# Decode attention with an MLP gate on one core: 68 of the 128 row pairs of heads 28 and 29 of the output weights load through GpSimd's queue, ahead of time, on two pairs of DMA engines

## The chip, the cores and the metric

The kernel runs on one core of a Trainium2 chip. A core has five engines with instruction streams of their own: PE (TensorE, matrix multiplication), DVE (VectorE), ACT (ScalarE), POOL (GpSimd) and SP (SyncE, which here does nothing but issue loads and stores), and 16 DMA engines that move data between the chip's memory (HBM) and the core's on-chip memory. SP, ACT and POOL can issue transfers, each into a queue of its own; the DMA engines work these queues off. Time is in microseconds (us) of the device; the metric is the median over several executions, lower is better.

## What is computed

One token passes through a block: a layer norm, attention of 32 heads over the last 4096 positions of a key and a value cache, and, beside it, a small MLP whose output gates the attention's.

```python
def _A_ref(x, k_cache, v_cache, wq, wo):          # x (1,1,512), caches (1,32,32768,128)
    W = min(4096, max(256, Sk // 4))              # 4096
    q = (x @ wq).reshape(B, Sq, Hq, Dh).transpose(0, 2, 1, 3)
    k = k_cache[:, :, Sk - W:, :]
    v = v_cache[:, :, Sk - W:, :]
    scores = einsum("bhqd,bhkd->bhqk", q, k) * (Dh ** -0.5)
    o = einsum("bhqk,bhkd->bhqd", softmax(scores), v)
    return o.transpose(0, 2, 1, 3).reshape(B, Sq, Hq * Dh) @ wo    # wo (4096, 512)
...
xn = _layernorm(x)
return x + _A_ref(xn, ...) * _silu(_B_ref(xn, ...))
```

Everything is bfloat16. The caches' windows are 32 MB each for K and V and must be read once: they are nearly all of the kernel's traffic.

## The kernel before

**Groups and steps.** The 32 heads are worked in eight groups of four (`G`). One group's keys are 4096 KB, laid out as 128 partitions by 128 chunks by 128 numbers, so that each partition gets one piece of 32 KB; one group's values likewise. The loop runs over ten steps `s`. In step `s` the keys of group `s` are loaded and multiplied with the query, half of them on DVE (`k_vector`: a product and a reduction, four parts) and half on PE (`k_turn` transposes, ACT copies the result out, `k_scores` multiplies). The softmax of group `s-1` follows (`sm_max`, `sm_turn`, `sm_exp`), and in the same step the values of group `h = s-2` are multiplied with its probabilities (`v_wide`, `v_turn`, `v_add`, `v_out`). `sm_den` and `sm_rden` make the reciprocal `rden` of a group's softmax sum; in step 6 that is group 4's.

**The output weights.** `wo` has a row block of 128 rows by 512 for each head. Heads 0 to 15, 16 to 23 and 24 to 27 are loaded as three blocks and used by `y_wide`. Heads 28 to 31 belong to the last group, whose output comes last; their rows are loaded into the tile `wo_rows` (128 partitions, 4 heads, 512 numbers, so 1 KB for a head in each partition), by two loads of two heads each (`load_rows`). They are the last loads in SP's queue, behind the last group's values. `y_head` multiplies them, four small matmuls a head, into `y_ps`.

**Who issues what.** SP issues nearly all loads, in the order of the program (`load`, line 76). A load into a buffer that is still read waits for that reader, and everything that SP is to issue later waits behind it. There are three buffers for keys and two for values. ACT issues the query weights and the input at the start. `mark` issues tiny loads: `marks` of k rows of 32 bytes for k = 1, 3, 5, 7 behind the last keys and for 9, 11, 13, 15 behind the `wo` blocks. GpSimd issues no transfers; its last instruction is the second `ln_rstd`, at 12 us.

**The tail.** Steps 8 and 9 have no keys. In step 9 the last values come in three cuts (chunks 0 to 64, 64 to 96 and 96 to 128). PE's order there is written by hand: `v_open`, three `warm` matmuls on zeros, `v_wide` on the first cut, the block of heads 24 to 27 (`ox_pick`, `y_wide`), `v_wide` on the second cut, `v_turn`, the sum of the earlier heads into `y_ps` (`rows_add`), `v_part` on the third cut (32 matmuls), then, once DVE has scaled the result (`v_out`), `y_head` for heads 28 to 31: 16 matmuls. DVE multiplies by the gate, adds the input, and SP stores 512 numbers.

`warm` matmuls write a PSUM tile that nobody reads.

Of the kernel before, what the change touches and what calls it, by code (L numbers as in the profile page):

```python
# [8 lines left out]
P = 128  # L9
BF16 = mybir.dt.bfloat16  # L10
FP32 = mybir.dt.float32
# [7 lines left out]
G = 4  # L19
LAG = 2  # L20
K_BUFS = 3
V_BUFS = 2
LATE = 7


@with_exitstack
def kernel(
# [14 lines left out]
    nc = tc.nc  # L42
# [3 lines left out]
    _, H, Sk, Dh = A_k_cache.shape  # L46
# [17 lines left out]
    small = ctx.enter_context(tc.tile_pool(name="small", bufs=1))  # L64
# [10 lines left out]
    def load(dst, src):  # L75
        return tc.keep_in_program_order(nc.sync.dma_start(out=dst, in_=src))  # L76
# [8 lines left out]
                        in_=A_wq.rearrange("(a b c) n -> b a (c n)", a=4, c=KC))  # L85
# [27 lines left out]
    zero_bf = const.tile([P, P], BF16, name="zero_bf")  # L113
# [95 lines left out]
    for b in range(2):  # L209
        zeros(qr[b][:])  # L210
        for c in range(KC):
            wc = wq_sb[:, c, :].rearrange("p (g a d) -> p g a d", a=G, d=Dh)
            for a in range(G):
                nc.tensor.matmul(qr[b][32 * a:32 * a + 1], lhsT=xq_bf[:, c:c + 1], rhs=wc[:, 4 * b:4 * b + 4, a, :],  # L214
                                 start=False, stop=(c == KC - 1), skip_group_check=True)
    nc.scalar.copy(out=q_row[:, 0:4, 0, :], in_=qr[0][:])
    nc.vector.tensor_copy(out=q_row[:, 4:8, 0, :], in_=qr[1][:])  # L217
    for b in range(2):
        qb_ps = ps_tr.tile([P, 4, Dh], FP32, tag="pt", name="qb_ps")
        nc.tensor.matmul(qb_ps[:], lhsT=sel[:].rearrange("k b a -> k (b a)"), rhs=q_row[:, 4 * b:4 * b + 4, 0, :],  # L220
                         start=True, stop=True)
        nc.scalar.copy(out=q_bc[:, 4 * b:4 * b + 4, :], in_=qb_ps[:])
    for b in range(2):
# [5 lines left out]
        for t in range(2):  # L229
            rows = slice(64 * t, 64 * t + 64)  # L230
            nc.scalar.copy(out=q_pair[rows, 4 * b:4 * b + 4, :, G * t:G * t + G].rearrange("p g l a -> p g a l"),
                           in_=qt_ps[rows].bitcast(BF16).rearrange("p g (a m l) -> p g a m l", a=G, l=2)[:, :, :, 0, :])
# [4 lines left out]
    for j in range(KC):  # L237
        for c in range(KC):
            nc.tensor.matmul(hs_ps[:, j:j + 1], lhsT=w2_sb[:, c, j::4],
                             rhs=shifted_bf[:, c:c + 1], start=(c == 0), stop=(c == KC - 1))  # L240
# [30 lines left out]
    for i in range(11):  # L271
        n = P if i < 10 else 96
        terms.append((a_bf[0:n, i % 3, i // 3:i // 3 + 1], w4_sb[0:n, i, :]))
    for i, (col, w) in enumerate(terms):
        r = 32 * (i % 4)
        nc.tensor.matmul(hr_ps[r:r + 1].rearrange("r j n -> r (j n)"), lhsT=col, rhs=w, start=False,
                         stop=(i >= len(terms) - 4), skip_group_check=True)
# [34 lines left out]
    st = {}  # L312

    def nd(g):
        return 64 if g == 0 or g >= LATE else 80

# [85 lines left out]
    def sm_rden(g):  # L402
        s = st[g]
        s["rden"] = sm_pool.tile([P, G], FP32, tag="rden", name="rden")
        nc.vector.reciprocal(out=s["rden"][:], in_=s["den"][:])  # L405
# [4 lines left out]
    h_part = H - G  # L410
# [6 lines left out]
    def wo_row(h):  # L417
        return wo_rows[:, h - h_part, :]

    def load_rows(h, n):  # L420
        load(wo_rows[:, h - h_part:h - h_part + n, :],
             A_wo[h * P:(h + n) * P, :].rearrange("(h p) n -> p h n", p=P))

    ov = ps_o.tile([P, 4, Dh], FP32, name="ov")
    zeros(ov[:])
# [82 lines left out]
    def warm(n):  # L510
        wm = ps_s.tile([P, 4, P], FP32, tag="sT", name="wm")
        for _ in range(n):
            nc.tensor.matmul(wm[:], lhsT=zero_bf[:], rhs=zero_bf[:].unsqueeze(1).to_broadcast([P, 4, P]),
                             start=True, stop=True)

    def y_open():
        yr[0] = ps_tr.tile([P, KC, P], FP32, tag="pt", name="yr_ps")
        zeros(yr[0][:])
# [18 lines left out]
    for s in range(NG + LAG):  # L537
        h = s - LAG
        last = h == NG - 1
        kn = load_kv(k_pool, A_k_cache, s, (0, 64, CP) if s == 0 else (0, CP)) if s < NG else None  # L540
        if s == NG - 1:
            mark((1, 3, 5, 7))
        if s == LAG:
            wts_guard.__exit__(None, None, None)
            v_pool = ctx.enter_context(tc.tile_pool(name="v", bufs=V_BUFS))
            wo_blk[2] = v_pool.tile([P, 4, D], BF16, tag="wo_4", bufs=1, name="wo_4")
            wo_rows = v_pool.tile([P, H - h_part, D], BF16, tag="wo_rows", bufs=1, name="wo_rows")
        if last:
            v = load_kv(v_pool, A_v_cache, h, cuts)
            for r in (H - G, H - 2):  # L550
                load_rows(r, 2)
        elif h >= 0:
            v = load_kv(v_pool, A_v_cache, h)
        if h == 3:
            wo_24 = k_pool.tile([P, 32, D], BF16, tag="kv", name="wo_24")
            wo_blk[0], wo_blk[1] = wo_24[:, 0:16, :], wo_24[:, 16:24, :]
            load_wo(0)
        if h == 5:
            load_wo(1)
            load_wo(2)  # L560
            mark((9, 11, 13, 15))

        if s < NG:
            nb = len(batches(s))

            def keys(b0, b1):
                for b in range(b0, b1):
                    k_turn(s, kn, b)
                    if b > 0:
                        k_scores(s, b - 1)  # L570

            k_open(s)
            k_vector(s, kn, 0)
            keys(0, 2)
            if s == 7:
                v_turn(h - 1)
                v_add(h - 1)
                v_out(h - 1)
            elif s > 1:
                sm_den(s - 2)  # L580
                sm_rden(s - 2)
            elif s == 1:
                sm_max(0)
            k_vector(s, kn, 1)
            keys(2, 4)
            if s == 7:
                sm_den(h)
                sm_rden(h)
                keys(4, nb - 2)
                sm_turn(s - 1)  # L590
                keys(nb - 2, nb)
            else:
                if s > 0:
                    sm_turn(s - 1)
                keys(4, nb)
            k_scores(s, nb - 1)
            sm_own(s)
            if s == 7:
                k_vector(s, kn, 2)
                v_wide(h, v)  # L600
                sm_exp(s - 1)
                v_turn(h)
                y_open()
                k_vector(s, kn, 3)
                v_add(h)
                v_out(h)
                ox_spread(1)
                sm_max(s)
                continue
            if s > 0:  # L610
                sm_exp(s - 1)
            if h > 0:
                v_turn(h - 1)
            k_vector(s, kn, 2)
            if h >= 0:
                v_wide(h, v)
            if h > 0:
                v_add(h - 1)
                v_out(h - 1)
            if s == 6:  # L620
                ox_spread(0)
            k_vector(s, kn, 3)
            if s == 6:
                ox_pick(0)
            if s > 0:
                sm_max(s)
        elif s == NG:
            ox_pick(1)
            sm_turn(NG - 1)
            sm_exp(NG - 1)  # L630
            y_wide(1, False)
            sm_den(NG - 2)
            sm_rden(NG - 2)
            y_wide(0, False)
            warm(3)
            v_wide(h, v)
            sm_den(NG - 1)
            sm_rden(NG - 1)
            v_turn(h)
            v_add(h)  # L640
            v_out(h)
            ox_spread(2)
        else:
            v_open(h)
            warm(3)
            v_wide(h, v, cuts[1], last=False)
            ox_pick(2)
            y_wide(2, True)
            nc.scalar.copy(out=y_sum[:], in_=yr[0][:].rearrange("p j n -> p (j n)"))
            v_wide(h, v, cuts[2], cuts[1])  # L650
            v_turn(h)
            v_add(h)
            rows_add(y_ps, ind, y_sum, False)
            v_part(h, v, cuts[2], CP)
            v_out(h)
            for r in range(H - G, H):
                y_head(r)
# [36 lines left out]
```

## Time and profile before

| | us |
|---|---|
| median of three runs (193.39 to 193.83) | 193.8 |
| time of the profiled execution | 193.51 |
| its span on the core | 191.3 |
| DVE busy | 150.9 |
| PE busy | 118.0 |
| ACT busy | 89.2 |
| last `v_part` begins / first `y_head` matmul / store issued | 186.22 / 187.47 / 188.77 |

The page of a profile gives, among other things, the busy time of each engine, a row of 40 equal slices with the busy share of the DMA engines in tenths, the queues (packets, MB, share of the time of 16 DMA engines), and the chain of waits: from the last instruction back to what released it, and so on. In the chain's list each line is a start, a length and what ran. The timeline lists instructions in order: start, length, engine, line of the code, operation, what it writes and reads, and in brackets how long the engine had been idle and what ended that. An "x15" counts instructions. The trace also holds a record of every DMA packet, with its queue, size, start and length.

### The profile page before, as it was taken

Reading aid. Unit: us, or ns where it says so; the run is one execution under the profiler, and the core shown is the slowest. Engines: PE = TensorE matmul, PEld = TensorE weight load, DVE = VectorE, ACT = ScalarE, POOL = GpSimd, SP = SyncE. Lnnn points to the kernel's source line nnn. Section 1 sums busy time; section 2 is a strip of 40 time slices with the busy share of each in tenths; the row PEclk is TensorE's granted clock in tenths of the full one; section 3 lists DMA queues with packets and bytes.
Section 4 is the critical chain, followed back from the end, with each engine's and each line's share of the span. In section 5 each row is a group of like instructions: output and inputs, shape, how many; then the busy total and the mean of one; then the engine's idle time right before and its main releaser. Section 6 shows DMA issues by size and latency. Waiting matters only on the chain.

```text
span 191.3 us, 2847 instructions
## 1 busy us (share of the span) xinstructions
PE 118.0 (62%) x1159; PEld 74.9 (39%) x1159; DVE 150.9 (79%) x175; ACT 89.2 (47%) x191; POOL 2.3 (1%) x11
## 2 busy tenths in 40 slices
PE   1554753989825368256845772680989289739762
PEld 0430222767614334143434442540864077313321
DVE  1660159979999999999999999999999999980111
ACT  2001370887794076427364564542575148734120
POOL 2110000000000000000000000000000000000000
PEclk9999695555755557955695588557555858975995
DMA  6999999999999999999999999999999998999990
GB/s 204 440 444 403 441 418 428 439 439 437 432 440 439 425 435 432 432 439 439 428 432 425 425 421 404 452 432 435 439 439 433 435 432 379 472 425 404 416 367 26
DMA packets 4700, 79.02 MB, mean 413 GB/s; under 512 B 752, under 2 KB 1360, under 8 KB 1616
## 3 DMA queue, kind: packets, MB, share of 16 engines
q1 hardware_dynamic: 4392, 74.65, 91.5%
q10 hardware_dynamic: 296, 4.20, 5.1%
q8 instruction: 9, 0.15, 0.3%
q14 instruction: 3, 0.02, 0.0%
HBM read 78.84 MB, written 0.00 MB: 412 GB/s over the span
## 4 chain that ended last, share of the span: by engine, by line
DVE 46%; DMA 43%; PE 6%; ACT 2%; issue 1%; SPq 1%; ACTq 0%; DVEq 0%
DMA kv<-in_A_k_cache_dram 31%; DVE S L329 28%; DVE prod L327 15%; DMA kv<-in_A_v_cache_dram 10%; DMA x_bf<-in_A_x_dram 2%; PE pt L345 2%; ACT kt L348 2%; PE ov L433 1%; PE sT L356 1%; DVE m L372 1%; SPq L76 1%; DVE S L370 1%; PE oT L467 1%; DVE mx L380 1%; PE ot_ps L450 0%
## 5 line engine op out<-in xcount | busy, mean ns | idle before, releaser
L329 DVE TENSOR_REDUCE S<-prod 128x20 f32<-128x2560 bf16 (+1 forms) x32 | 86.0, 2686 | 1.1
L348 ACT COPY kt<-pt 128x1024 bf16<-128x1024 bf16 x52 | 51.2, 1013 | 39.6 <-PE pt L345 37.9
L345 PE MATMUL pt<-ident_f,kv 128*128 128x128 f32 x208 | 46.8, 376 | 10.5 <-DMA kv<-in_A_k_cache_dram 10.5
L327 DVE TENSOR_TENSOR prod<-kv,q_bc 128x2560 bf16<-128x2560 bf16 (+1 forms) x32 | 45.4, 1417 | 3.8 <-DMA kv<-in_A_k_cache_dram 3.6
L345 PEld LDWEIGHTS pt<-ident_f,kv 128*128 128x128 f32 x208 | 34.3, 196 | 14.0 <-DMA kv<-in_A_k_cache_dram 9.7
L356 PE MATMUL sT<-q_pair,kt 128*128 128x8 bf16 x416 | 19.5, 170 | 15.6 <-ACT kt L348 15.5
L356 PEld LDWEIGHTS <-kt 128*128 128x128 bf16 x416 | 16.5, 105 | 26.7 <-ACT kt L348 25.7
L433 PE MATMUL ov<-kv,pT 128*16 128x512 bf16 x248 | 22.4, 523 | 1.2 <-DMA kv<-in_A_v_cache_dram 1.2
L394 ACT ACTIVATE pT<-S,mb 128x128 bf16<-128x128 f32 x32 | 14.0, 574 | 0.3
L378 PE MATMUL mt_ps<-ident_f,m 128*1 128x128 f32 x8 | 2.9, 360 | 17.3 <-DVE rden L405 16.8
L439 ACT COPY ov_sb<-ov 128x512 f32<-128x512 f32 x8 | 4.7, 586 | 18.1 <-PE ov L433 18.1
L433 PEld LDWEIGHTS <-pT 128*16 128x16 bf16 x248 | 6.8, 110 | 13.8 <-issue 12.0
L365 ACT ACTIVATE own<-sT,par 128x48 f32<-128x48 f32 (+1 forms) x32 | 7.5, 355 | 3.7 <-PE sT L356 3.7
L450 PE MATMUL ot_ps<-ident_f,ov_sb 128*128 128x128 f32 x32 | 7.5, 377 | 2.7 <-ACT mb L390 1.7
L217 DVE CAST q_row<-qr_ps 128x512 bf16<-128x512 f32 x1 | 0.7, 691 | 9.9 <-PE qr_ps L214 9.9
L394 ACT ACTIVATION_READ_ACCUMULATOR pT<-S,mb 128x1 f32 x32 | 8.3, 260 | 0.0
L378 PEld LDWEIGHTS mt_ps<-ident_f,m 128*1 128x1 f32 x8 | 0.6, 80 | 17.8 <-DVE rden L405 17.1
L405 DVE RECIPROCAL rden<-den_ps 128x4 f32<-128x4 f32 x8 | 1.4, 175 | 7.1 <-PE den_ps L400 7.1
L387 PE MATMUL mb_ps<-md,par_t 5*128 5x4 f32 x16 | 4.1, 323 | 4.1 <-DVE md L382 4.1
L450 PEld LDWEIGHTS ot_ps<-ident_f,ov_sb 128*128 128x128 f32 x32 | 4.8, 188 | 3.8 <-ACT mb L390 2.1
L261 ACT ACTIVATE a_row<-a_ps 128x384 bf16<-128x384 f32 x1 | 0.5, 490 | 12.1 <-remote 12.1
L387 PEld LDWEIGHTS mb_ps<-md,par_t 5*128 5x128 f32 x16 | 3.6, 275 | 5.1 <-PE sT L356 3.7
(122 smaller groups left out, 81.9 us busy)
## 6 DMA issues: line engine op xcount, KB each, us to landing
kv<-in_A_k_cache_dram SPq DMA_DIRECT2D x7, 4096.0 KB, 25.5
kv<-in_A_v_cache_dram SPq DMA_DIRECT2D x7, 4096.0 KB, 30.6
wq_sb<-in_A_wq_dram ACTq DMA_DIRECT2D x1, 4096.0 KB, 17.5
kv<-in_A_k_cache_dram SPq DMA_DIRECT2D x2, 2048.0 KB
wo<-in_A_wo_dram SPq DMA_DIRECT2D x1, 2048.0 KB
kv<-in_A_v_cache_dram SPq DMA_DIRECT2D x1, 2048.0 KB
kv<-in_A_v_cache_dram SPq DMA_DIRECT2D x2, 1024.0 KB, 17.6
w_sb<-in_B_w_dram SPq DMA_DIRECT2D x1, 1376.0 KB, 10.1
```

Of the source, the lines that this page charges most:

```text
L327: nc.vector.tensor_tensor(out=prod[:, 0:m, :], in0=kn[:, rows, :], in1=q_bc[:, g:g + 1, :].to_broadcast([P, m, Dh]), op=ALU.mult)
L329: nc.vector.tensor_reduce(out=st[g]["S"][:, rows], in_=prod[:, 0:m, :], axis=AX.X, op=ALU.add)
L345: nc.tensor.transpose(pt[:, i, :], kn[:, c:c + 2, :].rearrange("p c d -> p (c d)").bitcast(FP32), ident_f[:])
L348: nc.scalar.copy(out=kts[b][:, 0:n, :], in_=pt[:, 0:n, :].bitcast(BF16))
L356: nc.tensor.matmul(st[g]["sT"][:, c:c + 2, :].rearrange("p c a -> p (c a)"), lhsT=kt[:, i, l::2], rhs=q_pair[:, g, l, :], start=(l == 0), ...
L365: nc.scalar.mul(s["own"][:, 0:m, a], s["sT"][:, 0:m, a], par[:, a:a + 1])
L378: nc.tensor.transpose(mt_ps[:], s["m1"][:], ident_f[:])
L387: nc.tensor.matmul(mb_ps[:], lhsT=par_t[:].rearrange("k b a -> k (b a)"), rhs=md[:], start=True, stop=True)
L394: nc.scalar.activation(out=s["pT"][:, :, a], in_=s["S"][:], func=ACT.Exp, scale=scale, bias=mb[:, a:a + 1], accum_out=s["sum"][:, a:a + 1])
L433: nc.tensor.matmul(ov[r:r + 4 * G], lhsT=s["pT"][:, c:c + 4, :].rearrange("p i a -> p (i a)"), rhs=v[:, c:c + 4, :], start=(i < 4), stop=( ...
L439: nc.scalar.copy(out=s["ov_sb"][:], in_=ov[:])
L450: nc.tensor.transpose(ot_ps[:, step * j:step * j + P], s["ov_sb"][:, j, :], ident_f[:])
```

## The change

A new constant `ARC = 34`. Two tiles are added, `skip` and `gate`. In step 6, after `rden` of group 4 is issued, GpSimd copies that `rden` into `gate`, and then issues five loads: a tiny one of 7 rows, 34 partitions of heads 28 and 29 (partitions 0 to 33), a tiny one of 6 rows, the next 34 partitions (34 to 67), and a tiny one of 15 rows. A tiny row is two runs of 16 bytes. SP's load of heads 28 and 29 shrinks to partitions 68 to 127; its load of heads 30 and 31 stays. In step 9 the third `warm` matmul takes as its right side the first 68 partitions of head 28's rows in place of zeros (its left side is still zeros), so that it waits for GpSimd's two larger loads.

```diff
+ARC = 34
...
-    def load_rows(h, n):
-        load(wo_rows[:, h - h_part:h - h_part + n, :],
-             A_wo[h * P:(h + n) * P, :].rearrange("(h p) n -> p h n", p=P))
+    def rows_of(h, n, p0, p1):
+        return (wo_rows[p0:p1, h - h_part:h - h_part + n, :],
+                A_wo[h * P:(h + n) * P, :].rearrange("(h p) n -> p h n", p=P)[p0:p1])
+
+    def load_rows(h, n, p0, p1):
+        load(*rows_of(h, n, p0, p1))
+
+    skip = small.tile([16, 3, 2, 16], BF16, name="skip")
+    gate = small.tile([P, G], FP32, name="gate")
+
+    def load_arcs(g):
+        tc.keep_in_program_order(nc.gpsimd.tensor_copy(out=gate[:], in_=st[g]["rden"][:]))
+
+        def step(i, k):
+            tc.keep_in_program_order(nc.gpsimd.dma_start(
+                out=skip[0:k, i, :, 0:8], in_=A_x[0, 0, :].rearrange("(k t n) -> k t n", t=2, n=16)[0:k, :, 0:8]))
+
+        step(0, 7)
+        for i, k in enumerate((6, 15)):
+            dst, rows = rows_of(H - G, 2, ARC * i, ARC * i + ARC)
+            tc.keep_in_program_order(nc.gpsimd.dma_start(out=dst, in_=rows))
+            step(1 + i, k)
...
+        return wm
...
-            for r in (H - G, H - 2):
-                load_rows(r, 2)
+            load_rows(H - G, 2, 2 * ARC, P)
+            load_rows(H - 2, 2, 0, P)
...
+                if s == 6:
+                    load_arcs(s - 2)
...
-            warm(3)
+            wm = warm(2)
+            nc.tensor.matmul(wm[:].rearrange("p j n -> p (j n)"), lhsT=zero_bf[0:2 * ARC, :],
+                             rhs=wo_rows[0:2 * ARC, 0, :], start=True, stop=True)
```

## The prediction

> **What bounds the kernel now.** The page first: its DMA row and the queues.
>
> ```profile
> PE 118.0 (62%) x1159; PEld 74.9 (39%) x1159; DVE 150.9 (79%) x175; ACT 89.2 (47%) x191; POOL 2.3 (1%) x11
> ...
> DMA  6999999999999999999999999999999998999990
> ...
> q1 hardware_dynamic: 4392, 74.65, 91.5%
> q10 hardware_dynamic: 296, 4.20, 5.1%
> q8 instruction: 9, 0.15, 0.3%
> ...
> HBM read 78.84 MB, written 0.00 MB: 412 GB/s over the span
> ```
>
> The DMA engines are at 9 tenths or more from the second slice to the end of the loads, and POOL has next to nothing to do. The mean rate over stretches says how full: 1.00 of the engines' time from 40 to 130 us at 431 GB/s, 0.99 from 130 to 185.8. So DVE's 79%, which leads the chain of waits by share, is work beside a full stream of loads; the end is set by the stream. The last part of the chain, in order of time, shows it:
>
> ```profile
> 167.70 18.47 DMA kv<-in_A_v_cache_dram
> 186.17 0.05 issue
> 186.22 1.01 PE oT L467 x32
> 187.22 0.02 issue
> 187.25 0.17 DVE o L477
> 187.42 0.04 issue
> 187.47 0.64 PE y_ps L161 x15
> 188.10 0.02 issue
> 188.13 0.30 DVE y L660
> ```
>
> Eighteen microseconds of V load (the last cut of the last group), then only what cannot start before it: 32 matmuls, the scaling, 16 matmuls with wo_rows, two DVE steps, the store.
>
> Next the packet records, below the page. A packet starts 3 or 4 ns before the one ahead of it on its engine ends, so they can be strung into 16 chains, one for each DMA engine (the records do not name engines). From 49 us on the chains have no gap; a 32 KB packet takes 1213 to 1222 ns in all of them. They end the last V cut at these times: six at 184.04 to 184.19 us, one at 185.05, one at 185.37, eight at 185.56 to 185.85. What separates them is in the records too: eight of the nine 16 KB packets of queue 8 (instruction fetches) come before that end, and the seven of them that can be placed lie one each in seven of the last eight chains; 8 KB packets of queue 14 lie in the chains that end at 185.05 and 185.37. Around a fetch the chain loses 1.4 to 1.5 us: it takes 1006 to 1098 ns where the 16 KB packets of queue 1 take 611, and the next 32 KB packet takes 1.68 to 1.76 us. **The end is set by the chains that carried a fetch, and the six others have about 1.7 us to spare.** The 32-byte packets of `mark` tell chains apart: the four that hold 0, 8, 4 and 4 of them are among the six.
>
> **The change, part by part.** The profiled execution has a span of 191.3 us and a time of 193.51; the three runs have a median of 193.8, 0.3 above it.
>
> *Removed from SP's stream:* the first wo_rows load shrinks from 128 to 60 row pairs on 15 engines: 16 rows of 1 KB on each become 8, none on the sixteenth. Rows of 1 KB start 42 to 43 ns apart in the chains, so 8 x 42.5 = 0.34 us less. It lies behind the last V cut, so it moves only what follows: the second wo_rows load, whose last packet ends at 187.21. Who waits for that? The last 16 matmuls come as four groups of four: at 187.465, 187.525, 187.695 and 187.755. Two groups of a load stand 60 ns apart, but the third, the first to need the second load, starts 170 ns after the second. So wo_rows costs 0.11 us of waiting now. It started 0.48 us after the last packet's end; 0.34 us earlier (and 0.05 later, below) it would be ready at 187.40, before `o` lets the first group go at 187.465. Gain 0.11 us. The bound from the other side, with all four groups held by the load alone, is 187.695 - 187.465 = 0.23 us.
>
> *Added on four engines:* 34 row pairs on two engines are 17 pairs, 34 KB, on each: 34 x 42.5 ns = 1.45 us. If the queue deals its rows to consecutive engines, the small loads of 7, 6 and 15 rows put the two pairs on the eighth and ninth and on the sixteenth and first, which are the four chains above (4, 4, 0 and 8 marks). They end the last V cut at 184.04 to 184.19; plus 1.45 plus the small loads gives 185.5 to 185.7, under 185.85. Cost nothing, hidden by the slow chains. The cover is thin: (185.85 - 184.19) / 34 = 49 ns a row; beyond it every ns a row costs 0.034 us at the end.
>
> The nearest rows for the price of a row: 42.5 ns back to back in queue 1; and where two queues share an engine, as q1 and q10 do from 6.2 to 21 us, packets alternate one by one and the 478 of them are lengthened by 495 ns in all, 1 ns each, at a mean of 435 GB/s. The far row is the fetch, which stops its neighbour by 0.37 to 0.66 us (queue 14) once for each packet; 34 such stops would be 13 to 22 us. I take 43 ns, because rows out of a standing queue are nearest to q10.
>
> The Trainium skill, "DMA: Bandwidth & Descriptors", section "Why a DMA increments its semaphore by 16 and not by 1", has GpSimd's queue deal to k consecutive engines from a round-robin cursor, with k the largest divisor up to 16: 2 for 34 rows, 7, 6 and 15 for the small loads, which gives these pairs if the cursor starts at the first engine; no run here shows it yet.
>
> *Small loads on all the others:* `step` puts two 16-byte packets on each engine that it touches, and every delayed chain gets two such steps. A mark (32 bytes and its 4-byte completion) adds 12 ns to a chain. Four packets and up to five completion writes at 6 ns: 0.05 us, ahead of the last V cut, so on the path: +0.05. From above, if each of the two steps stops the engine as a queue 14 packet does: 2 x 0.37 to 2 x 0.66 = 0.74 to 1.32 us. I take the low end, by the row that has small loads of one queue in another's stream: x_bf's 8-byte packets lengthened q1's by 0.86 us over 16 engines between 2.85 and 4.3 us, 0.05 each.
>
> *GpSimd's work:* it waits for `rden` of group 4:
>
> ```profile
> 138.33 0.17 DVE L405 RECIPROCAL rden<-den_ps 128x4 f32<-128x4 f32 x1
> ```
>
> then one copy (its nearest, L184, takes 0.55 us) and five issues (SP's take 0.53 each): to 141.8. Nothing else is on that engine until the end. With one row for each packet of queue 1, 34 packets pass: K7, V5, wo1, wo2 are 32 of them and end at 164.6; the rows are down by about 169. PE asks for them in the changed third `warm` matmul:
>
> ```profile
> 179.72 0.81 PE L513 MATMUL wm<-zero_bf 128*128 128x512 bf16 x3
> ...
> 181.34 1.04 PE L433 MATMUL ov<-kv,pT 128*16 128x512 bf16 x16 [0.81 <-DMA kv<-in_A_v_cache_dram]
> ```
>
> Behind it on PE stand v_wide and all the tail, but v_wide waits for V7 until 181.34 anyway, so 12 us hide the loads and 0.8 us the matmul's own wait. If the copy or the issues slow DVE (3.3 us at worst), the last pT is ready at 174.3 for a V that lands at 180.9: hidden. K7 has been issued by then (130.37). Extra waits in SP's tail (62 ns each) fit into the 0.7 us in which it waits for the store.
>
> *Sum:* -0.11 + 0.05 = -0.06 on 193.51, and 193.7 against the median.
>
> **Rivals.**
>
> *Stalls by the new queue.* An engine drops its stream for a small load as it does for a fetch. For it: queue 14's 8 KB packets took 309 to 325 ns, no more than queue 1's, yet the next packet was 0.37 to 0.66 us longer, and neither of the queues that stall is of the page's kind hardware_dynamic, as q1 and q10 are; which kind GpSimd's is, no trace here shows. Against: q10's small packets, above. It is on the path from the first stop on, since the delayed chains have no slack. Two steps at 0.5 us: +1.0, with the 0.11 gained: 194.6. If all five loads stop every engine, 5 x 0.37 = 1.85: 195.5.
>
> *The four engines become the last.* Either the rows cost over 49 ns, or a pair sits on a delayed chain (another start of the dealing, a fetch on one of the four). On a delayed chain: 185.85 + 1.45 = 187.30, +1.45, so 195.2. At 70 ns a row: 184.19 + 2.38 + 0.1 = 186.67, +0.8: 194.5. For it: the placement is nowhere in this trace. Against: four of four fit the unhit chains. The Trainium skill, same page, "Latency and other measured facts", calls engines 7 and 15 usually slower, and this specific to GpSimd's queue, whose descriptor rings share their ports; by that rule two of the four engines would be the ones to overrun, with the 194.5 of the 70 ns row, and I give it 0.05 of this rival's 0.16. In this trace, without that queue, the chains with the marks of engines 7 and 15 are among the fast six.
>
> *The rows arrive late.* If they came after 181.3, PE would stand with the whole tail behind it: about 1 us for each late us. It takes over 12 us more than worked out: 3 in 100, some 195.
>
> *Faster by more than the wait.* The last V cut itself would have to land earlier on the slow chains; the change takes no byte from ahead of it there. It needs a fetch to move away from them: ending by 193.1 or less.
>
> **Chances.** Forecast 0.46; stalls 0.26; four engines last 0.16; late rows 0.03; faster 0.09. A measurement of this kernel can tell about 0.3% (0.6 us) from no change. Faster 0.09, same 0.46, slower 0.45. The likeliest alone: 193.3 to 194.1. The range over all: 193.2 to 195.3, which takes in both main rivals' centres and leaves out the five-fold stop, rows that each stop the engine, and part of the faster case.
>
> **What would show it.** Right: the last V cut lands at 185.8 to 185.95 with 14 or more chains within the last microsecond; the third group of the last matmuls follows the second by 60 ns; the wm matmul takes no wait beyond 181.3. Stalls: 32 KB packets over 1.5 us behind 16-byte packets after 139 us on most chains. Four engines last: the latest ends of the V cut are on chains that hold 34 extra 1 KB rows. Wrong altogether: the V cut landing before 185.5.

## The result and the profile after

The changed kernel takes 195.97 us (median of four runs, 195.81 to 196.27) beside 193.69 for the kernel before (four runs, 193.39 to 193.83): 1.0122 times as long, 95% interval 1.0104 to 1.0140. It is 2.28 us slower, and it lies above the predicted range. One run of all that follow, 206.23 us in the kernel with the even partitions, was in a slow state and is left out of its ratio.

The page of the changed kernel, its DMA row and its queues, the lines that were shown of before:

```profile
PE 122.1 (63%) x1159; PEld 78.4 (40%) x1159; DVE 151.2 (78%) x175; ACT 89.4 (46%) x191; POOL 7.5 (4%) x17
...
DMA  6999999999999999999999999999999999999990
...
DMA packets 4979, 79.02 MB, mean 406 GB/s; under 512 B 1131, under 2 KB 1603, under 8 KB 1895
...
q1 hardware_dynamic: 4255, 74.51, 91.3%
q10 hardware_dynamic: 296, 4.20, 5.1%
q0 software_dynamic: 416, 0.14, 0.3%
q8 instruction: 9, 0.15, 0.3%
...
HBM read 78.84 MB, written 0.00 MB: 405 GB/s over the span
```

The same bytes come over at 405 GB/s instead of 412. A new queue, q0, has 416 packets for 0.14 MB. The rows themselves are 36 packets (below) and the tiny loads have 28 rows between them; 416 is far more, and it is 26 times 16. The queue's own packets take 0.3% of the engines' time, 0.6 us; the loss is four times that. So the loss isn't in what the queue moves. It is in what it does to its neighbours, or elsewhere.

The chain of waits of the changed kernel, its last part in order of time (start, length, what ran):

```profile
170.07 19.23 DMA kv<-in_A_v_cache_dram
189.30 0.05 issue
189.35 1.03 PE oT L485 x32
190.38 0.02 issue
190.40 0.17 DVE o L495
190.57 0.04 issue
190.62 0.63 PE y_ps L162 x15
```

The chain has the shape that it had before. From the first of the 32 matmuls to the first matmul with the output weights is 1.27 us, before 1.25. All that was lost is lost ahead of 189.35, in the stream of V. The last 8 KB packet of V ends at 188.47 us, before at 185.84; by the chain the load has landed at 189.30 (170.07 + 19.23), before at 186.17. So 2.6 us are lost up to the last packet, and 0.5 us between it and the landing.

Where in the stream? A view by stretches of time, before and then after (stretch, length, busy time of PE, PEld, DVE, ACT and POOL with instructions, granted clock of PE, share of the DMA engines, GB/s). Of before:

```profile
95.00:137.00 42.00, 23.68 (x238) 15.79 (x237) 41.19 (x33) 21.68 (x51) 0.00 (x0) 0.70 1.01 432
140.00:172.00 32.00, 21.53 (x216) 13.90 (x215) 30.30 (x36) 16.73 (x39) 0.00 (x0) 0.71 1.01 434
```

Of after:

```profile
95.00:137.00 42.00, 24.54 (x229) 15.90 (x230) 40.79 (x33) 20.78 (x50) 0.00 (x0) 0.64 1.00 429
140.00:172.00 32.00, 22.81 (x221) 15.57 (x217) 29.77 (x32) 17.41 (x39) 4.34 (x6) 0.62 1.01 405
```

Read the last two columns. From 140 to 172 us, the time in which GpSimd's loads are at work, the engines are as full as before and move 7% less: (434 - 405) / 434 of 32 us is 2.1 us of stream. And from 95 to 137 us, when GpSimd has not issued anything yet, the rate is already 429 instead of 432.

The packet records of the changed kernel, strung into 16 chains as in the prediction, say what fills the engines. This is a stretch of one chain that carries none of the rows (start in us, queue, bytes, length in ns):

```
146.818  q1  32768  1241
148.056  q0     16    11
148.063  q1  32768  1285
149.344  q0     16    11
149.351  q1  32768  1401
```

A 32 KB packet takes 1213 ns before. Here 16-byte packets of the new queue stand between SP's packets, and each 32 KB packet behind one is longer: 118 ns on the mean of 117 of them (over 1216 ns). Counted by size, q0 has 32 packets of 4096 bytes and 4 of 2048 (the rows, on four engines), 28 of 32 bytes (the tiny rows), 224 of 16 bytes, 48 of 8 and 80 of 4. **Every one of the five loads puts as many packets on each of the 16 engines as its busiest engine has**: for 34 row pairs nine packets with data on two engines, and nine of 16 or 8 bytes on each of the 14 others (called fillers from here on), and a completion on all; for a tiny load one and a completion. 2 x 10 + 3 x 2 = 26 on each engine.

Last, where the stream's stages end on the chains. The load of group 6's values ends, over the 16 chains, at 174.26 to 176.07 us before. After, three chains end it at 176.70 to 176.85 and thirteen at 177.95 to 178.43, among them, as far as the stringing tells, all four that carried rows. So the four engines are no later than the nine others, and the whole stream is late. But the rows are not hidden either. Before, seven chains end the load by 174.42, the four that were to carry rows among them; after, only three end it early. By this count the rows' engines moved by at least 3.5 us (177.95 - 174.42), where the prediction worked out 1.5 and had 1.7 to spare. Some 0.6 us of it are the moved tiles, told below.

One caution for the absolute times that follow. The part of the time that lies outside the span is 2.1 to 2.3 us in every run of the kernel before, and 1.7 to 1.9 in every run of the changed kernel and of the thirteen below, also where GpSimd loads nothing. So inside the span each of them loses some 0.35 us more than its time says (the changed kernel's median span is 194.2 us, that of the kernel before 191.2 to 191.4). No run here shows why. Kernels of the same time also differ by 0.5 us in when a stage ends. Sizes therefore come from the medians of the times and from differences within one trace.

### The profile page after: what moved, and what is told of

The parts are those of the page before. It is cut to its first block, busy times and chain, and to the rows that moved or that the text cites. A ratio compares the mean times of both kernels' runs of the same rounds, so it can differ in the third digit from the quotient of the medians.

```text
span 194.5 us, 2859 instructions
## 1 busy us (share of the span) xinstructions
PE 122.1 (63%) x1159; PEld 78.4 (40%) x1159; DVE 151.2 (78%) x175; ACT 89.4 (46%) x191; POOL 7.5 (4%) x17
## 4 chain that ended last, share of the span: by engine, by line
DVE 46%; DMA 43%; PE 6%; ACT 1%; issue 1%; SPq 1%; DVEq 0%; ACTq 0%
DMA kv<-in_A_k_cache_dram 31%; DVE S L330 28%; DVE prod L328 15%; DMA kv<-in_A_v_cache_dram 10%; PE pt L346 2%; DMA x_bf<-in_A_x_dram 2%; ACT kt L349 1%; PE ov L451 1%; PE sT L357 1%; DVE m L373 1%; DVE S L371 1%; SPq L77 1%; DVE mx L381 1%; PE oT L485 1%; PE ot_ps L468 0%
## 5 line engine op out<-in xcount | busy, mean ns | idle before, releaser
L346 PE MATMUL pt<-ident_f,kv 128*128 128x128 f32 x208 | 50.2, 399 | 10.7 <-DMA kv<-in_A_k_cache_dram 10.7
L346 PEld LDWEIGHTS pt<-ident_f,kv 128*128 128x128 f32 x208 | 37.1, 209 | 14.3 <-DMA kv<-in_A_k_cache_dram 10.3
L451 PE MATMUL ov<-kv,pT 128*16 128x512 bf16 x248 | 22.9, 531 | 2.4 <-DMA kv<-in_A_v_cache_dram 2.4
L432 POOL COPY gate<-rden 128x4 f32<-128x4 f32 x1 | 1.4, 1417 | 126.0 <-DVE rden L406 126.0
```

The lines of the kernel that those rows point to most:

```text
L346: nc.tensor.transpose(pt[:, i, :], kn[:, c:c + 2, :].rearrange("p c d -> p (c d)").bitcast(FP32), ident_f[:])
L451: nc.tensor.matmul(ov[r:r + 4 * G], lhsT=s["pT"][:, c:c + 4, :].rearrange("p i a -> p (i a)"), rhs=v[:, c:c + 4, :], start=(i < 4), stop=( ...
```

## The experiments

Thirteen kernels were run. They fall into three questions, in which order they are told here. All ratios are to the kernel before, run on the same chip in turn with them.

### Which part costs: tiny loads, the rows, the copy?

**Five loads that are all tiny.** The two loads of rows become tiny rows; SP loads all 128 row pairs.

```diff
-            dst, rows = rows_of(H - G, 2, ARC * i, ARC * i + ARC)
-            tc.keep_in_program_order(nc.gpsimd.dma_start(out=dst, in_=rows))
+            step(3 + i, 2)
...
-            load_rows(H - G, 2, 2 * ARC, P)
+            load_rows(H - G, 2, 0, P)
...
+            warm(3)
```

> Five GpSimd loads at the same place and on the same engines, but the two larger ones carry 2 rows of 32 bytes each; SP loads all of wo_rows, as before. Theory 'turns' (each packet of GpSimd's queue that takes a turn between SP's packets costs its engine some 0.05 to 0.13 us, and every engine gets as many packets as the busiest one, 26 with the change, 10 here): 10 packets of 4 to 32 bytes at about 0.05 us, so 0.4 to 0.6 us over before, 194.1 to 194.3. Theory 'loads' (a fixed cost of about 0.48 us for each GpSimd load on every engine, 2.4 us in all): as slow as the change, 195.9 to 196.1. Theory 'four engines' (the engines with the 34 KB became the last, the rest costs nothing): 193.7 to 193.8.

193.94 us, 1.0025 (1.0015 to 1.0035). The ten packets that each engine gets (160 in q0) lengthen the 32 KB packets behind them by 9 ns (4 bytes), 24 ns (8 bytes) and 14 ns (32 bytes). Five loads from this queue don't stop an engine five times. The time lies under what the theory 'turns' expected, and the kernel with the copy alone, below, takes as long, so the five tiny loads add nothing that the runs can tell.

**Half as many rows by GpSimd.** The two loads carry head 28's rows only, SP loads the rest.

```diff
-            dst, rows = rows_of(H - G, 2, ARC * i, ARC * i + ARC)
+            dst, rows = rows_of(H - G, 1, ARC * i, ARC * i + ARC)
...
-            load_rows(H - G, 2, 2 * ARC, P)
+            load_rows(H - G, 1, 2 * ARC, P)
+            load_rows(H - G + 1, 1, 0, P)
```

> The two larger GpSimd loads carry head 28 alone (34 rows of 1 KB, 17 KB on each of the four engines), SP loads the rest of head 28 and all of head 29. Turns: each larger load now makes 5 packets and a completion on every engine where it made 9 and one, so 18 in place of 26: 0.5 for the small part and 8 of 16 fillers at 0.12, 1.45 us over before, 195.0 to 195.3. Loads: five loads still, 195.8 to 196.1. Four engines: 17 KB is 0.72 us less on them, so under 194.6.

195.59 us, 1.0109 (1.0091 to 1.0127): little less than the whole change, but by another way, so that it does not answer the question. The rows are not on two pairs of engines any more. q0 has 160 packets, 22 of them of 3072 bytes: a load of 34 rows of one head is dealt three rows to an engine, over twelve engines. A 3072-byte packet takes 128 ns and makes the 32 KB packet behind it 188 ns longer, and all of these rows go to partitions 0 to 67. What that means is told with the loads that are spread over 16 engines, below.

**Other engines for the rows.** Tiny loads of 3, 6 and 3 rows move the two pairs.

```diff
-        step(0, 7)
-        for i, k in enumerate((6, 15)):
+        step(0, 3)
+        for i, k in enumerate((6, 3)):
```

> The change with small loads of 3, 6 and 3 rows in place of 7, 6 and 15: if the queue deals rows to consecutive engines, the two pairs move from the eighth and ninth and sixteenth and first engine to the fourth and fifth and the twelfth and thirteenth. The packets on each engine are as many as with the change. Turns, with the prediction's reading of the engines: the twelfth and thirteenth carry an instruction fetch each and have no slack, so the end moves by the 34 KB, 1.45 us, and by what the larger packets cost more than fillers (9 x 0.03), on top of the change's 2.3: 197.3 to 197.8. If the fillers alone made the change slow and the place of the 34 KB does not matter: 195.9 to 196.1.

197.61 us, 1.0242 (1.0175 to 1.0309; three runs of 197.50 to 197.62 and one of 200.28): by the medians 1.6 us more than the change. Group 6's values now end at 178.85, 179.24 and 179.26 us on three chains and by 178.07 on all others. The dealing follows the sizes of the tiny loads, and a pair of engines without slack costs about what the prediction worked out for it (1.45). Why three chains are that late, and not two, is open. Five chains now end the load early, by 176.92, where the change has three, as it must be if only two of the engines with rows now belong to the early seven. So the change had its rows where they were meant to be, on the engines with the most slack.

**The copy alone.** GpSimd copies `rden`, and loads nothing.

```diff
-        step(0, 7)
-        for i, k in enumerate((6, 15)):
...
-            step(1 + i, k)
...
-            load_rows(H - G, 2, 2 * ARC, P)
+            load_rows(H - G, 2, 0, P)
...
+            warm(3)
```

> GpSimd waits for rden and copies it, but issues no load; SP loads all of wo_rows, as before. All three theories: as before, 193.5 to 193.9. If GpSimd's wait and copy beside DVE were what cost the time: up to 195.9.

194.02 us, 1.0024 (1.0013 to 1.0034), the same as the five tiny loads, and over what all three theories expected. Nothing is loaded by GpSimd, and 0.42 us are gone, in a kernel that has only a copy and two small tiles more. The stretches of this run:

```profile
95.00:137.00 42.00, 23.47 (x234) 15.38 (x235) 40.72 (x33) 21.18 (x51) 0.00 (x0) 0.64 1.00 428
140.00:172.00 32.00, 21.51 (x217) 13.52 (x215) 30.63 (x36) 17.00 (x39) 0.46 (x1) 0.77 1.00 428
```

The rate is down in the first stretch already, well before the copy. The tiles `skip` and `gate` have moved what is allocated after them by 224 bytes in each partition: both V buffers begin at byte 160512 before, a multiple of 256, and at 160736 after, 32 past a multiple of 64. In the V load of this trace's last stage the packets take, as medians, 1216, 614 and 313 ns (32, 16 and 8 KB); before 1213, 611 and 309. It is 3 or 4 ns a packet, whatever its size. But the place of the written buffer can't be the whole account. The keys' buffers are allocated ahead of the two tiles and have not moved, and the keys' 32 KB packets are longer too: as medians 1216 or 1217 ns in groups 3, 4 and 5, before 1213. How the shift does it stays open.

The Trainium skill, "DMA: Bandwidth & Descriptors", section "How a descriptor splits into AXI transactions", has a piece that does not begin at a multiple of 256 bytes split into transactions with a partly used first one. It says so of reads; here it is the written side that moved. The trace does not bear the 256 out for this side: the keys' buffers begin 128 past a multiple of 256 in the kernel before, and their packets take the same 1213 ns as those of V.

**The change with its tiles back in place.** The tile `pad`, which the kernel before has already, grows by 144 elements, so that the V buffers start 256 past a multiple of 512 as before.

```diff
-    small.tile([P, 96], BF16, name="pad")
+    small.tile([P, 240], BF16, name="pad")
```

> The change with 288 bytes more of padding, so that the value, query-weight and wo tiles lie a whole 512 bytes further than before, where skip and gate had moved them by 224 (from a multiple of 64 to 32 beyond one). Theory 'place' (the 0.42 us of the copy-only kernel is that shift: each value packet of 32, 16 and 8 KB some 3 to 10 ns longer): 0.3 to 0.5 us under the change, 195.3 to 195.6. If the copy itself or GpSimd's presence cost the 0.42: as the change, 195.9 to 196.1.

195.43 us, 1.0096 (1.0069 to 1.0123), 0.54 under the change by the medians, though the intervals touch. The V packets of the last stage are 1213, 611 and 309 ns again, the keys' are back at 1213, and so is the rate ahead of GpSimd's loads:

```profile
95.00:137.00 42.00, 24.11 (x237) 15.90 (x238) 41.15 (x33) 21.62 (x50) 0.00 (x0) 0.65 1.00 431
```

So the moved tiles are the cause, by whatever way, and not the copy, which is still there (three kernels below with the pad and the copy are at 1.0006 to 1.0010). This kernel is called the aligned change below. All kernels that follow have the pad, but for two that are marked.

### The middle: rows and fillers

**Rows by GpSimd, and all rows again by SP.** This was to show GpSimd's loads without the smaller SP load.

```diff
-            load_rows(H - G, 2, 2 * ARC, P)
+            load_rows(H - G, 2, 0, P)
```

> Padded as f1; GpSimd issues the change's five loads, and SP loads all 128 row pairs as before, on 16 engines. Theory 'turns': the packets in the middle of the stream cost the slow chains about 1.6 us: 195.1 to 195.4, and what the aligned change takes more than this is the tail on 15 engines. If the middle costs nothing that reaches the end and it is all in the tail: 193.6 to 193.8.

201.86 us, 1.0435 (1.0411 to 1.0460): a mistake in the edit, not a measurement of the loads. The timeline (start, length, what ran, in brackets the idle time and who ended it):

```profile
181.07 0.59 PE L531 MATMUL wm<-zero_bf 128*128 128x512 bf16 x2
188.38 0.58 PE L667 MATMUL wm<-wo_rows,zero_bf 68*128 68x512 bf16 x1 [6.71 <-DMA wo_rows<-in_A_wo_dram]
188.89 1.46 PE L451 MATMUL ov<-kv,pT 128*16 128x512 bf16 x12
```

The third `warm` matmul now waits for SP's load too, which is the last of all, and `v_wide` stands behind it for 6.71 us. What it shows is the price of the late-rows rival: PE stands 6.71 us, and the kernel is 7.1 us longer than the same one without the wait, which comes next.

**The same without the wait.**

```diff
-            wm = warm(2)
...
-                             rhs=wo_rows[0:2 * ARC, 0, :], start=True, stop=True)
+            warm(3)
```

> As the arcs-only kernel, with three plain warm matmuls, so that PE does not wait for SP's rows in the middle of its work: the change's five GpSimd loads, and SP's loads as before. The middle of the stream alone: 1.4 to 1.7 us over before, 194.9 to 195.2 (the last chain of V6 ended 1.39 us later in the arcs-only kernel and 1.67 in the aligned change). If the tail made most of it: 193.6 to 194.2.

194.72 us, 1.0063 (1.0046 to 1.0080), a little under the forecast: 1.22 us for GpSimd's five loads beside an untouched SP stream and untouched places. In the view by stretches it has the changed kernel's middle:

```profile
140.00:172.00 32.00, 21.20 (x214) 13.42 (x212) 30.26 (x36) 16.62 (x39) 3.63 (x5) 0.71 1.01 407
```

A 32 KB packet behind a 16-byte one is 110 ns longer (121 of them), behind 4 bytes 44, behind 8 bytes 43. From the end of group 6's values to the last 8 KB packet of V it takes 9.77 us, as before, so the tail has no part in this loss. The 32 KB packets behind GpSimd's are longer by 18 us over the 16 engines, 1.1 us on each, and the queue's own packets take 0.6 us on each. Inside the span the kernel loses 1.5 us (192.9, before 191.4), so these packets are enough to account for it.

**The same rows spread over the partitions.** Is it where the rows are written? The rows go to every third partition.

```diff
-            dst, rows = rows_of(H - G, 2, ARC * i, ARC * i + ARC)
-            tc.keep_in_program_order(nc.gpsimd.dma_start(out=dst, in_=rows))
+            dst, rows = rows_of(H - G, 2, i, i + 3 * ARC - 2)
+            tc.keep_in_program_order(nc.gpsimd.dma_start(out=dst[::3], in_=rows[::3]))
```

> As the kernel with the five loads, SP's loads as before and three plain warm matmuls (194.7, 1.0063 of before), but each larger GpSimd load takes every third partition (0, 3, ... 99 and 1, 4, ... 100) in place of 0 to 33 and 34 to 67. Same packets, fillers, bytes and engines. Theory 'fillers and turns' (the cost in the middle is the 26 packets on every engine, wherever the rows go): 194.5 to 194.9. Theory 'the same partitions' (the rows get in the way of the streams that write the same part of the partition range, and spread out they share it among more engines): 194.0 to 194.3, and the excess behind a 4 KB packet and behind a filler about halves.

194.41 us, 1.0062 (1.0039 to 1.0086, with one run of 195.59 in it): between the two forecasts, and no clear difference. The medians are 1.04 us over the runs of before, 1.15 for the rows in one place. A 32 KB packet behind a 16-byte one is 81 ns longer (117 of them) where it was 110, behind 4 KB 55 where it was 71. So the place of the rows is at most a part; most of the loss stays as long as the other engines get their fillers.

**One engine's rows and one tiny load.** 17 row pairs on a single engine, then a tiny load of 15 rows: 12 packets on each engine.

```diff
-        step(0, 7)
-        for i, k in enumerate((6, 15)):
-            dst, rows = rows_of(H - G, 2, ARC * i, ARC * i + ARC)
-            tc.keep_in_program_order(nc.gpsimd.dma_start(out=dst, in_=rows))
-            step(1 + i, k)
+        dst, rows = rows_of(H - G, 2, 0, 17)
+        tc.keep_in_program_order(nc.gpsimd.dma_start(out=dst, in_=rows))
+        step(0, 15)
```

> Padded; GpSimd loads 17 row pairs on one engine and a small load of 15 rows; SP's loads as before. One engine gets nine packets with data, the 15 others eight packets of 16 bytes and one of 8. Theory 'fillers' (a packet of 16 bytes costs its engine some 0.1 us of the following 32 KB packet by itself): 0.6 to 0.9 us over before, 194.1 to 194.4. If they cost only because 136 KB of rows get in the way of other engines at the same time: 0.2 or less, 193.5 to 193.7.

193.75 us, 1.0010 (0.9993 to 1.0026): unclear, a loss of 0 to 0.5 us. The records show 55 ns behind a 16-byte packet (95 of them), half of the 110 above. So a filler has no one price, and what sets it stays open.

### Spread over all 16 engines: the place of the rows, and the tail

**One load of 64 row pairs, partitions 0 to 63, on all 16 engines.** SP loads the upper half. (Without the pad.)

```diff
-        step(0, 7)
-        for i, k in enumerate((6, 15)):
...
+        dst, rows = rows_of(H - G, 2, 0, 64)
+        tc.keep_in_program_order(nc.gpsimd.dma_start(out=dst, in_=rows))
...
-            load_rows(H - G, 2, 2 * ARC, P)
+            load_rows(H - G, 2, 64, P)
```

> One GpSimd load of 64 row pairs, 4 pairs (8 KB) on each of 16 engines, no small loads; SP loads the other 64. Turns: 2 packets of 4 KB and a completion on each engine, no fillers: 2 x 0.30 and 0.05 on the path, less 0.1 at the end: 0.5 to 0.6 us over before, 194.2 to 194.4. Loads: one load, 0.48, and 8 KB, 0.34, less 0.1: 194.4. Four engines: 0.34 less 0.1, 193.9. If GpSimd's part in the loads costs 2 us whatever its shape: 195.9.

195.91 us, 1.0127 (1.0110 to 1.0144), as slow as the change, with 48 packets in the queue instead of 416 and no fillers:

```profile
q0 software_dynamic: 48, 0.13, 0.2%
```

Each 4 KB packet costs its engine 593 ns on the mean ahead of a 32 KB one, its own 187 ns and 406 that the neighbour gets longer; there are two of them on each engine.

**The same load issued by ACT.** (Without the pad.)

```diff
+        tc.keep_in_program_order(nc.scalar.dma_start(out=dst, in_=rows))
```

> The same 64 row pairs, evenly over 16 engines, issued by ACT in place of GpSimd at the same place in the program. If a turn costs as much for any second queue: 8 packets of 1 KB and a completion at about 0.1 and the 8 KB itself (0.34), less 0.1, so 1.1 us over before, 194.8. If only GpSimd's queue costs so much: 0.34 and under 0.1 less 0.1, so 0.2 to 0.4 over before, 193.9 to 194.1.

195.84 us, 1.0124 (1.0108 to 1.0140). Here the rows are packets of 1 KB, eight on each engine, and each costs 144 ns with what the 32 KB packet behind it gets longer: 1.15 us, where the two 4 KB packets cost 1.19. So this cost does not belong to GpSimd's queue. Whether it belongs to the half of the partitions is tried next.

**The even partitions by GpSimd, the odd ones by SP.** (With the pad.)

```diff
+        dst, rows = rows_of(H - G, 2, 0, P)
+        tc.keep_in_program_order(nc.gpsimd.dma_start(out=dst[0:P:2], in_=rows[0:P:2]))
...
-            load_rows(H - G, 2, 2 * ARC, P)
+            dst, rows = rows_of(H - G, 2, 0, P)
+            load(dst[1:P:2], rows[1:P:2])
...
+            warm(3)
```

> Padded as f1; one GpSimd load of the 64 row pairs of the even partitions (4 pairs on each of 16 engines), SP loads the odd ones. So each engine's rows go to all parts of the partition range in both loads, where the 64-pair kernel had the lower half in the middle and the upper half at the end. Theory 'half the partitions': the 2.4 us of that kernel shrink to the 8 KB ahead of the last cut (0.34) and three turns (0.1 to 0.3) less 0.1: 193.9 to 194.2. Theory 'turns alone' (where the rows go does not matter): 0.42 less than that kernel, 195.4 to 195.6.

193.59 us, 1.0006 (0.9994 to 1.0019): as before. It moves 64 of 128 row pairs through GpSimd's queue, with the copy and the two tiles, and costs nothing that the time shows; inside the span it is 0.4 us longer (191.7). The 4 KB packets cost 155 ns, their own time alone. So where the rows go decides, but one thing is not separated: with every other partition the rows are also every other row of `wo` in HBM. The wait that the prediction wanted to take out of the last 16 matmuls is gone: their groups start at 188.532, 188.587, 188.642 and 188.697, 55 ns apart. But the kernel with one engine's rows has the same 55 ns, and there SP loads all 128 row pairs, so the smaller load is not shown to do it. This is the best of the changed versions, and no better than the kernel before.

**Only the tail.** GpSimd loads nothing; SP loads partitions 64 to 127 of heads 28 and 29, and `y_head` multiplies these alone for those heads. The lower half of their rows is left out of the result.

```diff
+        p0 = 64 if h < H - 2 else 0
...
-            load_rows(H - G, 2, 2 * ARC, P)
+            load_rows(H - G, 2, 64, P)
```

> Padded as f1; GpSimd issues no load. SP loads only partitions 64 to 127 of heads 28 and 29, 4 pairs on each of 16 engines, and y_head uses only these; the other half of the two heads' rows is left out. Theory 'half the partitions' (rows that all go to the upper partitions get in each other's and the last V cut's way): the 8 KB packets of the last cut and the 1 KB rows are lengthened as in the runs with the change, 0.2 to 0.7 us over before, 193.9 to 194.3. Theory 'less is less' (the prediction's): 0.1 under before, 193.4 to 193.6.

193.74 us, 1.0010 (0.9998 to 1.0021): about 0.26 us by the median, though the interval takes in no change, and 0.6 us inside the span (191.9, before 191.3). The timeline of this run:

```profile
185.67 0.40 PE L162 MATMUL y_ps<-y_sum,ind 128*1 128x128 f32 x8
186.82 0.97 PE L476 MATMUL oT<-pT,kv 128*128 128x4 bf16 x32 [0.75 <-DMA kv<-in_A_v_cache_dram]
```

and of the kernel before:

```profile
185.65 0.40 PE L161 MATMUL y_ps<-y_sum,ind 128*1 128x128 f32 x8
186.22 0.99 PE L467 MATMUL oT<-pT,kv 128*128 128x4 bf16 x32 [0.17 <-DMA kv<-in_A_v_cache_dram]
```

PE has come as far by the same time (185.67 and 185.65) and then waits 0.75 us for the last cut of V instead of 0.17, though there is less to load. The records say why, for a part: the fast engines have finished V and write the rows into the upper partitions, and meanwhile 8 KB packets of the last cut on the slow engines take up to 454 ns instead of 309. It takes 10.00 us from the end of group 6 to the last 8 KB packet, before 9.77. The rest comes after that packet: the load lands 0.71 us behind it, before 0.33. The aligned change has 10.01, up to 524 ns, and lands 0.62 us behind. The four kernels with the pad, and without the mistaken wait, in which SP's load of these rows goes to all 128 partitions or to every other one have 9.77, nothing above 320, and 0.34 to 0.38.

### The sum

| part | from | share | us |
|---|---|---|---|
| the moved tiles | copy alone, 1.0024 | 0.24% | 0.4 |
| GpSimd's loads beside SP's stream | rows without the wait, 1.0063 | 0.63% | 1.2 |
| SP's remaining rows in the upper partitions | aligned change less that, 1.0096 - 1.0063 | 0.33% | 0.6 |
| together | | 1.20% | 2.3 |
| the change | | 1.22% | 2.28 |

The first two are measured by themselves, and their intervals exclude no change. The third is a difference of two medians whose intervals touch. In the records 0.24 us of it are seen twice in the packets, and another 0.24 us (aligned change, 0.62 beside 0.38) and 0.37 us (tail alone, 0.71 beside 0.33) between the last packet of V and the landing; why the landing comes later is open. The time of the kernel with that part alone shows 0.26 (0 to 0.4). The sum is of times, and each of its kernels gains the unexplained 0.35 us outside the span once.

## Why the prediction was wrong

**What held.** The stream of V sets the end, and the chain behind it is unchanged. The slow engines are those that carried an instruction fetch; the rows sat on four of those with the most slack, and moving them costs 1.6 us. The rows came in time: their last packets on the four engines end between 157.7 and 166.7 us (169 was worked out), and the `wm` matmul that asks for them did not wait:

```profile
182.49 0.38 PE L667 MATMUL wm<-wo_rows,zero_bf 68*128 68x512 bf16 x1
183.82 1.04 PE L451 MATMUL ov<-kv,pT 128*16 128x512 bf16 x16 [0.95 <-DMA kv<-in_A_v_cache_dram]
```

It is the first cut of V that `v_wide` still waits for behind it. The hidden work on GpSimd was larger than said and still hidden; its timeline:

```profile
139.16 1.42 POOL L432 COPY gate<-rden 128x4 f32<-128x4 f32 x1 [126.05 <-DVE rden L406]
140.53 0.75 POOL L435 DMA_DIRECT2D skip<-in_A_x_dram  x1
141.27 0.98 POOL L441 DMA_DIRECT2D wo_rows<-in_A_wo_dram  x1
142.24 0.57 POOL L435 DMA_DIRECT2D skip<-in_A_x_dram  x1
142.80 0.98 POOL L441 DMA_DIRECT2D wo_rows<-in_A_wo_dram  x1
143.78 0.57 POOL L435 DMA_DIRECT2D skip<-in_A_x_dram  x1
```

The copy takes 1.42 us instead of 0.55, and the issues end 2.5 us later than worked out. DVE is busy for 151.2 us, before 150.9, so the copy did not slow it.

**"Small loads on all the others: +0.05."** This step failed. It counted four packets and up to five completions on a delayed chain at 6 ns. The loads of 34 row pairs were taken to touch only their two engines; in fact each puts nine packets on every other engine too, so there are 26, and 16 of them are of the dear kind: about half of these stand ahead of a 32 KB packet and make it about 110 ns longer. Measured: 1.22 us (0.9 to 1.5). The upper bound given for the term, 0.74 to 1.32 for two stops, has it inside, but for another reason: it is many small delays and not two large ones. The row that was chosen as nearest, the 8-byte packets of `x_bf`, comes from a time when q1's packets beside them are small. The five tiny loads alone do bear it out (9 to 24 ns).

**"Added on four engines: cost nothing."** This step failed too, though the time does not show it by itself, because all engines are late. The price of a row was taken as 42.5 ns, from rows back to back, and the cover was 49. In the changed kernel a 4 KB packet of rows takes 169 ns and makes the 32 KB packet behind it 133 ns longer, so a row costs some 75 ns, an estimate from these two numbers. The rows' engines moved by 3.5 us or more instead of 1.5, some 0.6 of it by the moved tiles (with the copy alone the seven early chains end at 174.86 to 175.14). It is not a fixed price: in the kernel with one engine's rows a 4 KB packet costs 159 ns, its own time alone. What the loss would be if the fillers cost nothing was not run; the prediction's own rival, at 70 ns a row, had 0.8 us for it.

**"Removed from SP's stream: -0.11."** The third group of the last matmuls follows the second by 106 ns in place of 170 (190.616, 190.676, 190.782, 190.889). That is no wait taken out by the smaller load: the fourth group follows by 107, and the kernel with the rows without the wait, in which SP loads all row pairs, has 106 and 107 as well. And the step took the rest of the load for a shorter version of the old one. It is a load into the upper partitions alone, and that holds up the last cut on other engines: 0.24 us seen in the packets and as much in the landing, about 0.6 by the medians. The sign was wrong.

**Not in the sum at all: the two new tiles.** `skip` and `gate` were costed as nothing, not even named as a cost, though the kernel before has a tile `pad` ahead of them that nobody reads. They move what is allocated after them, the V buffers too, and that is 0.42 us.

The largest of these is the small loads' 1.22 us. The rival nearest to the truth was "stalls by the new queue", at 194.6 for two stops (its own terms give 194.7) and 195.5 for five. Its mechanism for the price, an engine that drops its stream for every load, fell with the five tiny loads.

The sign that the prediction named for that rival, 32 KB packets of over 1.5 us behind 16-byte packets on most chains, is not what the trace shows either; 1.27 to 1.37 are typical, and 4 of 119 are over 1.5. A threshold set by the dearest row would have passed over the true cause.

## What to carry to other kernels

When a small load is put beside a stream that fills the engines, count its packets on every engine and not only on those that carry data, and ask which partitions it writes: 64 row pairs into every other partition cost nothing that the time shows, into one half of the partitions about 1% beyond what the moved tiles cost. And price a row by what it does to its neighbours, not by its own time: the slack of 1.7 us was no cover for 34 KB in the changed kernel. A tile added early in a pool moves everything allocated after it; compare the packet lengths of a stretch that lies before the change takes effect, as 95 to 137 us did here. And where the end is set by a full stream, its rate by stretches says at once in which part the time went, before any theory of how.

## What the runs showed of the hardware

- A load through GpSimd's queue that uses two engines puts a packet on each of the 16 for every packet of the busiest: 416 for two loads of 34 row pairs and three tiny ones. The Trainium skill, "DMA: Bandwidth & Descriptors", section "Why a DMA increments its semaphore by 16 and not by 1", has all 16 engines post a completion for this queue whatever the shape; the trace agrees (80 packets of 4 bytes for five loads). The 224 fillers of 16 bytes stand beside those completions.
- A 32 KB packet behind such a filler is 55 to 118 ns longer, while the filler itself takes 11. Why is open: the rows' partitions are at most a part of it (81 ns with spread rows), and it is not the queue's tiny packets as such (9 to 24 ns).
- A 4 KB packet of a load spread over 16 engines costs 593 ns when the rows go to partitions 0 to 63 and 155 ns when they go to every other partition, beside the same stream (the second kernel has the pad, and takes every other row of `wo`).
- With the V buffers moved from a multiple of 256 to 32 past a multiple of 64, their packets of 8 to 32 KB take 3 or 4 ns more each, and packets of keys into buffers that did not move about as much: 0.42 us in all.
- The last V load lands 0.33 to 0.38 us after its last packet where SP's next load writes all or every other partition, 0.62 and 0.71 us where it writes the upper ones alone (all of these with the buffers in place).
